# Capped attention and two expert layers on one core: attention in units of two key blocks, the shared block on half rows, seven pairs in float32

## The chip, the core and the metric

The kernel runs on one core of a Trainium2 chip. Its engines work side by side, each through its own queue in order: TensorE (PE, with its weight loads shown apart as PEld), VectorE (DVE), ScalarE (ACT), GpSimd (POOL) and SyncE (SP, which here issues the DMAs). The metric is the device time of one launch in microseconds.

## What is computed

```python
def _attn_ref(q, k, v, cap):                       # q, k, v: (2, 12, 448, 64)
    scores = np.matmul(q, k.transpose(0, 1, 3, 2)) / np.sqrt(64)
    scores = cap * np.tanh(scores / cap)
    attn = np.exp(scores - np.max(scores, axis=-1, keepdims=True))
    attn = attn / (np.sum(attn, axis=-1, keepdims=True) + 1e-09)
    return np.matmul(attn, v)
...
x = attn_out.transpose(0, 2, 1, 3).reshape(896, 768)
h = np.maximum(np.maximum(x @ w1, x @ w2), x @ w3)  # 768 x 768 each
y = h @ w_out
g = y @ w_in                                        # 768 x 2048
g = np.maximum(g, 0.0) + alpha * np.minimum(g, 0.0)
return g @ w_out2                                   # 2048 x 768
```

All is float32. The weights come as pairs of 32-bit words and are decoded on the chip.

## The kernel before

**Heads go in pairs.** The 24 heads are 12 pairs. In `qk` a pair's two heads lie on partitions 0 to 63 and 64 to 127, so that a score product of one head takes 64 rows of the array and the two heads' products lie beside each other. The 448 keys are cut into three blocks of 128 for both heads and one shared block: its 128 rows are the last 64 keys of the first head and, below, the last 64 of the second. `CHUNKS` (L142) lists 12 x 4 chunks: blocks 0, 1, 2 and the shared one (`None`).

**A chunk's steps.** `scores` (L251) makes the transposed scores (keys on partitions, 448 queries along the row) in a PSUM tile `sc`, two buffers, in three passes of rounded parts: high by high, high by low, low by high. `tanh` (L263) reads it on ACT into the tile `a`; `exp` (L269) works on `a` in place. No maximum is subtracted, since the cap bounds the scores. `weighted` (L284) multiplies with v: the stationary operand is 128 keys x 128 columns, 64 of v and 64 of ones, so that the same product gives the sum of the exponentials. In the pairs of `FULL` (L144: 1, 3, 5, 7, 9, 11) this is one float32 matmul for each head, which the trace shows as two instructions; in the other pairs `a` and v are split into a rounded part and a remainder (`a_high`, `a_low`, `v_high`, `v_low`, on DVE) and three passes are made. In the shared block each head's product takes all 128 rows, and zeros, written once by `beside` (L212), stand in v against the other head's keys.

**After a pair.** `taken` copies the two products from PSUM on ACT (`e`); `summed`, `inverted`, `in_row` and `spread` bring the sums by DMA into a column, invert them, and spread them over 64 partitions (`rc`, `row`, `rb`); `normal`, `x_high` and `x_low` give the normalised result, split in two parts, to the expert layers.

**Order.** Every step is a task with an engine, an estimated cost, what it must follow, and a key (`KEYS`, L186, in chunks from the chunk's number). `planned` (L146) goes through the tasks with these costs and emits them in the order of the planned start times; `in_order` then fixes that order for every queue. Buffers: `AB` 6 tiles `a`, `SB` and `LB` 4 tiles for the split parts, `PB` 2 PSUM tiles each for scores and products. Three weight blocks of the first expert layer are loaded and decoded inside attention (`GATES`, L184). Then `experts` (L511) begins with ten of the twelve pairs for all three weight blocks and takes the last two pairs at the end (`late`).

**The rest**, some 400 us, is matmuls of rounded parts in three passes (`product`, L94).

Of the kernel before, what the change touches and what calls it, by code (L numbers as in the profile page):

```python
# [10 lines left out]
F32 = mybir.dt.float32  # L11
F32R = mybir.dt.float32r
# [3 lines left out]
AF = mybir.ActivationFunctionType  # L16
# [14 lines left out]
def attention_moe_moe2(ctx: ExitStack, tc: tile.TileContext, t):  # L31
# [6 lines left out]
    KF, _, DM = t["w_in2"].shape  # L38
    KD = DM // P

    AB, SB, LB, PB = 6, 4, 4, 2

    WARM = 11

# [96 lines left out]

    CHUNKS = [(p, block) for p in range(PAIRS) for block in (0, 1, 2, None)]  # L142

    FULL = range(1, PAIRS, 2)  # L144

    def planned(tasks, start):  # L146

# [45 lines left out]
    def fast_attention(xh, xl, pools, begin):  # L193
# [78 lines left out]
        def a_high(i):  # L272
            a = splits[i]
            ah = work.tile([P, 2, S], F32R, name="ah", bufs=SB)[:, : a.shape[1]]
            rounded(ah, a, "DVE")
            splits[i] = a, ah

        def a_low(i):
            a, ah = splits[i]
            al = work.tile([P, 2, S], F32R, name="al", bufs=LB)[:, : a.shape[1]]  # L280
            remainder(al, a, ah)
            splits[i] = ah, al

        def weighted(i):  # L284
# [4 lines left out]
            for head in range(2):  # L289
                j = 0 if block is None else head  # L290
                out = pvs[p][:, head, :S]
                start, stop = block == 0, block is None
                cols = slice(head * P, (head + 1) * P)
                if p in FULL:
                    nc.tensor.matmul(out, values(p, "f")[:, c, cols], splits[i][:, j], start=start, stop=stop)  # L295
                    continue
                ah, al = splits[i]
                vh, vl = (values(p, part)[:, c, cols] for part in "hl")
                nc.tensor.matmul(out, vh, ah[:, j], start=start, stop=False)  # L299
                nc.tensor.matmul(out, vh, al[:, j], start=False, stop=False)  # L300
                nc.tensor.matmul(out, vl, ah[:, j], start=False, stop=stop)  # L301

        def taken(p, h):

            if h == 0:
                divisors[p] = small.tile([P, 2, S], F32, name="e"), small.tile([CP, 2, S // CP], F32, name="rc")
            nc.scalar.copy(out=divisors[p][0][:, h], in_=pvs[p][:, h, :S])  # L307

        def summed(p, h):
# [57 lines left out]
        splitting = [i for i in range(n) if CHUNKS[i][0] not in FULL]  # L367
        of = [[i for i in range(n) if CHUNKS[i][0] == p] for p in range(PAIRS)]
# [5 lines left out]
        for p in range(PAIRS):  # L374
# [4 lines left out]
            if p == 0:  # L379
                for x, (cols, dep) in enumerate(((slice(0, CUT), "KIN"), (slice(CUT, QK), "QIN"))):  # L380
                    m = cols.stop - cols.start
                    add(("XKH", 0, x), "DVE", rounding("DVE", m), [((dep, 0), 0.0)], -99 + x, qk_high, 0, cols, "DVE")
                    add(("XKL", 0, x), "DVE", low(m), [("XKH", 0, x)], -98.5 + x, qk_low, 0, cols)
            else:
                transfer(("Lx", p), 0.63, 2.6, past("XKL", p - 2, 0), s0 + KEYS["Lx"], load_qk, p)
                free = past("SC", of[p - 2][-1]) if p > 1 else []
# [9 lines left out]
            if not full:  # L396
# [5 lines left out]
            for i in of[p]:  # L402
                two = CHUNKS[i][1] is not None
                m = S * (2 if two else 1)
                deps = past("SC", i - 1) + past("TA", i - PB)
                deps += [("XKL", 0, 0 if i == 0 else 1)] if p == 0 else [("XKL", p, 0)]
                add(("SC", i), "PE", 0.75 if two else 0.61, deps, i + KEYS["SC"], scores, i)
                old = i - AB
                free = [] if old < 0 else past("PV", old) if CHUNKS[old][0] in FULL else past("AL", old)
                add(("TA", i), "ACT", 0.9 if two else 0.53, [("SC", i)] + free, i + KEYS["TA"], tanh, i)  # L410
                add(("EX", i), "ACT", 0.93 if two else 0.56, [("TA", i)], i + KEYS["EX"], exp, i)
                if full:
                    deps = [("EX", i)]
                    cost = 1.5
                else:
                    x = splitting.index(i)
                    free = past("PV", splitting[x - SB]) if x >= SB else []
                    add(("AH", i), "DVE", rounding("DVE", m), [("EX", i)] + free, i + KEYS["AH"], a_high, i)
                    free = past("PV", splitting[x - LB]) if x >= LB else []
                    add(("AL", i), "DVE", low(m), [("AH", i)] + free, i + KEYS["AL"], a_low, i)  # L420
                    deps = [("AL", i)]
                    cost = 1.22
                deps = deps + ready_v + past("PV", i - 1)
                deps += past("TKA", p - 2) + past("TKB", p - 2)
                add(("PV", i), "PE", cost, deps, i + KEYS["PV"], weighted, i)
# [15 lines left out]
        for w, gate in enumerate(GATES):  # L441
            stages = begin(w)
            step = lambda stages=stages: next(stages, None)
            free = [("EX", gate)]
            transfer(("WL", w), 0.4, 4.2, [("EX", max(0, gate - 8))] + past("W2", w - 2), 1000 + w * 10, step)
            times = (("ACT", 0.8), ("DVE", 1.05), ("DVE", 1.8), ("ACT", 0.8), ("DVE", 0.9))
            for j, (engine, cost) in enumerate(times):
                deps = [(("WL!", w), 0.3)] + free + past("W4", w - 2) if j == 0 else [(f"W{j - 1}", w)]
                add((f"W{j}", w), engine, cost, deps, 1000 + w * 10, step)
        anchors = {}  # L450
        for name in planned(tasks, 3.6):
            task, args = tasks[name][4]
            task(*args)
            if name in (("EX", n - 1), ("AL", splitting[-1]), ("PV", n - 1), ("DA", PAIRS - 1)):
                anchors[name[0]] = list(nc.cur_bb.bb.instructions)[-1]
        return list(anchors.values())

# [249 lines left out]
```

## Time and profile before

| | us |
|---|---|
| median of 3 runs (539.97 to 541.96) | 541.27 |
| the profiled execution, device time | 541.33 |
| its span in the trace | 539.3 |
| first score matmul | 6.08 |
| the attention's last product on PE ends, first expert matmul | about 117.9 |
| last wait of PE for attention's results ends | 137.87 |

The profile is of one execution. A row of the timeline gives start, duration, engine, line, operation, tiles, shape and how many equal instructions are merged; in brackets stands the idle time before it and what ended it. Matmuls are pipelined: a matmul's duration in the trace is longer than its share of the engine, so that share is read from the distances of starts.

### The profile page before, as it was taken

Reading aid. Unit: us, or ns where it says so; the run is one execution under the profiler, and the core shown is the slowest. Engines: PE = TensorE matmul, PEld = TensorE weight load, DVE = VectorE, ACT = ScalarE, POOL = GpSimd, SP = SyncE. Lnnn points to the kernel's source line nnn. Section 1 sums busy time; section 2 is a strip of 40 time slices with the busy share of each in tenths; the row PEclk is TensorE's granted clock in tenths of the full one; section 3 lists DMA queues with packets and bytes.
Section 4 is the critical chain, followed back from the end, with each engine's and each line's share of the span. In section 5 each row is a group of like instructions: output and inputs, shape, how many; then the busy total and the mean of one; then the engine's idle time right before and its main releaser. Section 6 shows DMA issues by size and latency. Waiting matters only on the chain.

```text
span 539.3 us, 6459 instructions
## 1 busy us (share of the span) xinstructions
PE 527.0 (98%) x2519; PEld 447.4 (83%) x2519; DVE 380.6 (71%) x512; ACT 233.2 (43%) x296; POOL 5.0 (1%) x20
## 2 busy tenths in 40 slices
PE   7999999999999999999999999999999999999995
PEld 3665566579899999999999999999999999999994
DVE  5768899754988767667666899999988665565300
ACT  5989999862444333233333233333333223223110
POOL 3000000000000000000000000000000000000000
PEclk9999999999999999999999999999999999999998
DMA  6456244115355332233333233322333344344001
GB/s 198 139 152 175 69 115 108 36 35 153 117 177 175 118 117 95 93 110 113 118 117 108 68 118 117 117 80 98 108 98 107 108 131 143 107 132 141 1 35 40
DMA packets 27350, 59.19 MB, mean 110 GB/s; under 512 B 14384, under 2 KB 17584, under 8 KB 27312
## 3 DMA queue, kind: packets, MB, share of 16 engines
q1 hardware_dynamic: 27312, 58.69, 35.3%
q8 instruction: 22, 0.36, 0.3%
q14 instruction: 16, 0.13, 0.1%
HBM read 55.85 MB, written 2.80 MB: 109 GB/s over the span
## 4 chain that ended last, share of the span: by engine, by line
PE 88%; ACT 4%; DVE 3%; DMA 2%; issue 1%; DVEq 0%; SPq 0%; ACTq 0%
PE acc L99 25%; PE acc L100 24%; PE acc L98 24%; PE pv L295 5%; PE sc L260 5%; PE pv L299 2%; ACT a L266 2%; PE pv L300 1%; PE pv L301 1%; DMA rb<-row 1%; ACT a L270 1%; DVE rb L336 1%; ACT e L307 1%; DMA cap_t<-in_cap 1%; DVE f L115 1%
## 5 line engine op out<-in xcount | busy, mean ns | idle before, releaser
L82 ACT CAST wh<-f 128x768 fp32r<-128x768 f32 (+1 forms) x58 | 47.2, 814 | 203.4 <-PE acc L99 195.2
L87 DVE TENSOR_TENSOR wl<-f,wh 128x768 fp32r<-128x768 f32 (+1 forms) x58 | 53.6, 925 | 52.5 <-ACT wh L82 52.3
L99 PE MATMUL acc<-xl,wh 128*128 128x448 f32 x216 | 79.0, 366 | 0.7 <-DVE xl L87 0.7
L98 PE MATMUL acc<-xh,wh 128*128 128x448 f32 x216 | 79.2, 367 | 0.0
L100 PE MATMUL acc<-xh,wl 128*128 128x448 f32 x216 | 78.9, 365 | 0.0
L108 ACT ACTIVATE f<-raw 128x768 f32<-128x768 f32 (+1 forms) x58 | 51.1, 881 | 55.0 <-DVE wl L87 39.1
L98 PE MATMUL acc<-yh,wh 128*128 128x448 f32 x192 | 70.7, 368 | 0.0
L99 PE MATMUL acc<-yl,wh 128*128 128x448 f32 x192 | 70.7, 368 | 0.0
L100 PE MATMUL acc<-yh,wl 128*128 128x448 f32 x192 | 70.7, 368 | 0.0
L98 PE MATMUL acc<-gh,wh 128*128 128x448 f32 x192 | 70.7, 368 | 0.0
L99 PE MATMUL acc<-gl,wh 128*128 128x448 f32 x192 | 70.7, 368 | 0.0
L100 PE MATMUL acc<-gh,wl 128*128 128x448 f32 x192 | 70.7, 368 | 0.0
L118 DVE SCALAR_TENSOR_TENSOR f<-raw,f 128x768 int32<-128x768 int32 (+1 forms) x58 | 53.9, 929 | 1.7
L115 DVE SCALAR_TENSOR_TENSOR f<-raw,f 128x768 int32<-128x768 int32 (+1 forms) x58 | 53.8, 928 | 1.4
L110 DVE TENSOR_SCALAR f<-f 128x768 f32<-128x768 f32 (+1 forms) x58 | 31.6, 545 | 25.5 <-ACT f L108 25.5
L266 ACT ACTIVATE a<-sc,s_in 128x896 f32<-128x896 f32 (+1 forms) x48 | 43.7, 918 | 9.6 <-PE sc L260 9.2
L270 ACT ACTIVATE a<-a,cap_t 128x896 f32<-128x896 f32 (+1 forms) x48 | 44.9, 955 | 0.4
L99 PEld LDWEIGHTS acc<-xl,wh 128*128 128x128 f32 x216 | 40.6, 188 | 4.5 <-DVE xl L87 1.1
L98 PEld LDWEIGHTS acc<-xh,wh 128*128 128x128 f32 x216 | 40.6, 188 | 3.4 <-PE pv L295 0.2
L100 PEld LDWEIGHTS acc<-xh,wl 128*128 128x128 f32 x216 | 40.6, 188 | 3.2
L295 PE MATMUL pv<-a,vf 128*128 128x448 f32 x96 | 40.5, 553 | 0.0
L99 PEld LDWEIGHTS acc<-yl,wh 128*128 128x128 f32 x192 | 36.0, 188 | 3.7
(70 smaller groups left out, 757.6 us busy)
## 6 DMA issues: line engine op xcount, KB each, us to landing
raw<-in_w SPq DMA_DIRECT2D x18, 768.0 KB, 4.4
raw<-in_w_in SPq DMA_DIRECT2D x16, 768.0 KB, 4.3
raw<-in_w_out SPq DMA_DIRECT2D x12, 768.0 KB, 4.4
raw<-in_w_out SPq DMA_DIRECT2D x12, 640.0 KB, 3.9
qkd<-in_qk SPq DMA_DIRECT2D x11, 480.0 KB, 3.8
rb<-row SPq DMA_DIRECT2D x24, 112.0 KB, 3.0
out<-ot SPq DMA_DIRECT2D x12, 224.0 KB, 2.8
vd<-in_v SPq DMA_DIRECT2D x6, 256.0 KB, 4.2
```

The lines of the kernel that those rows point to most:

```text
L82: nc.scalar.copy(out=hi, in_=src)
L87: nc.vector.tensor_tensor(out=lo, in0=src, in1=hi.bitcast(F32), op=ALU.subtract)
L98: nc.tensor.matmul(out, wh, xh, start=first and i == 0, stop=False)
L99: nc.tensor.matmul(out, wh, xl, start=False, stop=False)
L100: nc.tensor.matmul(out, wl, xh, start=False, stop=last and i == n - 1)
L108: nc.scalar.activation(out=f, in_=high.bitcast(F32), func=AF.Abs)
L110: nc.vector.tensor_scalar(out=f, in0=f, scalar1=WORD_MIN, scalar2=WORD_MAX, op0=ALU.max, op1=ALU.min)
L115: nc.vector.scalar_tensor_tensor(out=fi, in0=low, scalar=29, in1=fi, op0=ALU.logical_shift_right, op1=ALU.bitwise_or)
L118: nc.vector.scalar_tensor_tensor(out=fi, in0=high, scalar=-0x40000000, in1=fi, op0=ALU.bitwise_and, op1=ALU.bitwise_or)
L266: nc.scalar.activation(out=a, in_=sc, func=AF.Tanh, scale=s_in)
L270: nc.scalar.activation(out=splits[i], in_=splits[i], func=AF.Exp, scale=cap_t)
L295: nc.tensor.matmul(out, values(p, "f")[:, c, cols], splits[i][:, j], start=start, stop=stop)
```

## The change

Two neighbouring chunks become a unit: blocks 0 and 1 (four score tiles wide) and block 2 with the shared block (three wide). There are 24 units.

- The tile `a` is four wide. `tanh` still runs by chunk. `exp`, the split of `a` and the products with v run by unit; in the first two and the last two units (`FINE`) the exponentials and the products of the first chunk are steps of their own (`EA`, `PA`).
- The scores of a unit's second chunk get a key that puts them right behind those of the first.
- In the shared block each head's product with v takes only the 64 rows of its own keys, and the heads take turns. The zeros in v, and the four memsets of 64x64 in `h` and `f` for each buffer set, go.
- `FULL` becomes 0, 1, 3, 5, 7, 9, 11: pair 0 is no longer split.
- Buffers are halved in number (`AB` 3, `SB`, `LB` 2) and doubled in size; `e` and `rc` get three buffers, and `taken` follows the normalisation of the pair three before instead of two.
- Keys, gates and estimated costs are stated in units.

```diff
-    AB, SB, LB, PB = 6, 4, 4, 2
+    AB, SB, LB, PB = 3, 2, 2, 2
...
-    FULL = range(1, PAIRS, 2)
+    UNITS = [4, 3] * PAIRS
+    FINE = (0, 1, len(UNITS) - 2, len(UNITS) - 1)
+    FULL = [0, 1, 3, 5, 7, 9, 11]
...
-    GATES = (20, 27, 44)
+    GATES = (10, 13, 22)
     KEYS = dict(
-        Lx=-16, Lv=-12, XKH=-6, XKL=-5, VH=-3, VL=-2.5, TKA=4.2, TKB=4.3, INV=7, NM=8, XH=8.5, XL=9,
-        SC=-1.5, TA=-1, EX=0.5, AH=0.6, AL=0.7, PV=4,
+        Lx=-8, Lv=-6, XKH=-4, XKL=-3.9, VH=-1.5, VL=-1.2, TKA=1.9, TKB=2, INV=2.2, NM=2.7, XH=2.9, XL=3.2,
+        SC=-1.4, TA=-0.5, EX=0, AH=0.1, AL=0.2, PV=1.25,
     )
...
-            if part != "l":
-                nc.gpsimd.memset(v_[D:, 3, D : 2 * D], 0.0)
-                nc.gpsimd.memset(v_[:D, 3, 2 * D : 3 * D], 0.0)
...
         def tanh(i):
             sc = scs.pop(i)
-            a = work.tile([P, 2, S], F32, name="a", bufs=AB)[:, : sc.shape[1]]
-            nc.scalar.activation(out=a, in_=sc, func=AF.Tanh, scale=s_in)
-            splits[i] = a
+            if i % 2 == 0:
+                splits[i // 2] = work.tile([P, 4, S], F32, name="a", bufs=AB)
+            at = i % 2 * 2
+            nc.scalar.activation(out=splits[i // 2][:, at : at + sc.shape[1]], in_=sc, func=AF.Tanh, scale=s_in)
-        def exp(i):
-            nc.scalar.activation(out=splits[i], in_=splits[i], func=AF.Exp, scale=cap_t)
+        def exp(u, cols):
+            a = splits[u][:, cols]
+            nc.scalar.activation(out=a, in_=a, func=AF.Exp, scale=cap_t)
...
+            at = i % 2 * 2
+            if p in FULL:
+                terms = [(values(p, "f"), splits[i // 2])]
+            else:
+                (vh, vl), (ah, al) = (values(p, part) for part in "hl"), splits[i // 2]
+                terms = [(vh, ah), (vh, al), (vl, ah)]
+            def term(m, head):
+                v_, a_ = terms[m]
+                r = slice(head * D, (head + 1) * D) if block is None else slice(0, P)
+                j = at if block is None else at + head
+                start, stop = block == 0 and m == 0, block is None and m == len(terms) - 1
+                v_ = v_[r, c, head * P : (head + 1) * P]
+                nc.tensor.matmul(pvs[p][:, head, :S], v_, a_[r, j], start=start, stop=stop)
+            turns = [(m, head) for m in range(len(terms)) for head in range(2)]
+            for m, head in turns if block is None else sorted(turns, key=lambda x: x[1]):
+                term(m, head)
...
+                for i in (2 * u, 2 * u + 1):
+                    deps = past("SC", i - 1) + past("TA", 2 * u - 2) + past("TA", 2 * u - 1)
...
+                    add(("SC", i), "PE", cost, deps, u + KEYS["SC"] - i % 2 * 1000, scores, i)
...
+                if u in FINE:
+                    add(("EA", u), "ACT", 0.93, [("TA", 2 * u)], u + KEYS["EX"] - 0.3, exp, u, slice(0, 2))
+                cols = slice(2 if u in FINE else 0, UNITS[u])
+                cost = 0.17 + (cols.stop - cols.start) * S / 1200
+                add(("EX", u), "ACT", cost, [("TA", 2 * u), ("TA", 2 * u + 1)], u + KEYS["EX"], exp, u, cols)
...
+                if u in FINE:
+                    first_deps = [("EA", u)] + deps[1:]
+                    add(("PA", u), "PE", 1.6, first_deps, u + KEYS["PV"] - 0.2, weighted, chunks[:1])
+                    deps, chunks, cost = [("EX", u), ("PA", u)], chunks[1:], cost - 1.5
+                add(("PV", u), "PE", cost, deps, u + KEYS["PV"], weighted, chunks)
-            free = past("NA", p - 2) + past("NB", p - 2)
+            free = past("NA", p - 3) + past("NB", p - 3)
...
```

## Rows read from the trace of the kernel before

**Rows 1.** The profile's page: busy time by engine, and the chain that ended last.

```profile
PE 527.0 (98%) x2519; PEld 447.4 (83%) x2519; DVE 380.6 (71%) x512; ACT 233.2 (43%) x296; POOL 5.0 (1%) x20
PE 88%; ACT 4%; DVE 3%; DMA 2%; issue 1%; DVEq 0%; SPq 0%; ACTq 0%
```

**Rows 2.** Busy time by stage: stretch, length, PE, PEld, DVE, ACT, POOL, PE clock, DMA, GB/s.

```profile
6.08:117.90 111.82, 107.62 (x493) 67.68 (x493) 89.54 (x146) 99.81 (x131) 3.55 (x12) 1.00 0.43 118
117.90:137.90 20.00, 19.26 (x96) 17.50 (x94) 12.21 (x23) 5.65 (x10) 0.00 (x0) 1.00 0.51 153
137.90:538.00 400.10, 395.27 (x1922) 360.64 (x1922) 277.61 (x340) 126.29 (x154) 0.00 (x0) 1.00 0.33 106
```

**Rows 3.** Timeline of PE: start, duration, instruction; a float32 pair, and attention's end.

```profile
63.58 0.36 PE L260 MATMUL sc<-qkh,qkl 128*128 128x448 f32 x1
63.78 1.66 PE L295 MATMUL pv<-a,vf 128*128 128x448 f32 x4
65.38 0.47 PE L260 MATMUL sc<-qkh 64*128 64x448 f32 x2
65.69 0.37 PE L260 MATMUL sc<-qkl,qkh 64*128 64x448 f32 x2
65.89 0.36 PE L260 MATMUL sc<-qkh,qkl 64*128 64x448 f32 x2
66.18 1.77 PE L295 MATMUL pv<-a,vf 128*128 128x448 f32 x4
...
68.19 0.36 PE L260 MATMUL sc<-qkl,qkh 64*128 64x448 f32 x2
...
111.92 6.17 PE L295 MATMUL pv<-a,vf 128*128 128x448 f32 x16
...
118.13 0.36 PE L99 MATMUL acc<-xl,wh 128*128 128x448 f32 x1
```

**Rows 4.** Timeline of PE: its waits in attention, and first and last change of shape.

```profile
9.58 0.47 PE L260 MATMUL sc<-qkh 128*128 128x448 f32 x1
...
14.47 0.47 PE L260 MATMUL sc<-qkl,qkh 64*128 64x448 f32 x2 [0.50 <-DVE qkl L87]
...
78.14 0.47 PE L260 MATMUL sc<-qkh 128*128 128x448 f32 x1 [0.71 <-ACT a L266]
...
88.34 0.47 PE L260 MATMUL sc<-qkh 128*128 128x448 f32 x1 [0.89 <-ACT a L266]
...
106.36 0.47 PE L299 MATMUL pv<-ah,vh 128*128 128x448 f32 x1 [0.27 <-ACT e L307]
```

**Rows 5.** Timeline of ACT: exponentials of both widths and what follows them.

```profile
60.08 1.97 ACT L270 ACTIVATE a<-a,cap_t 128x896 f32<-128x896 f32 x2
61.95 0.99 ACT L266 ACTIVATE a<-sc,s_in 128x896 f32<-128x896 f32 x1
62.84 0.83 ACT L82 CAST wh<-f 128x768 fp32r<-128x768 f32 x1
...
75.61 0.68 ACT L270 ACTIVATE a<-a,cap_t 128x448 f32<-128x448 f32 x1
76.16 0.58 ACT L82 CAST xh<-rb 128x448 fp32r<-128x448 f32 x1
```

**Rows 6.** Waits of ACT from 6 to 118 us: in total, times, longest.

```profile
ACT a L266 <- PE sc L260: 9.2, 13, 3.3
```

**Rows 7.** First v load in float32: its issue on SP, and DMA issues of 0 to 30 us.

```profile
7.30 1.35 SPq L227 DMA_DIRECT2D vf<-in_v  x2
vf<-in_v SPq DMA_DIRECT2D x4, 128.0 KB, 4.8
```

**Rows 8.** Timeline of ACT and PE where the last two pairs are handed over.

```profile
110.75 1.65 ACT L270 ACTIVATE a<-a,cap_t 128x896 f32<-128x896 f32 x2
...
121.07 0.96 ACT L307 COPY e<-pv 128x448 f32<-128x448 f32 x2
137.87 0.47 PE L99 MATMUL acc<-xl,wh 128*128 128x448 f32 x1 [0.74 <-DVE xl L87]
```

More of the change, by code (lines that the diff above doesn't have):

```diff
@@ L264, in tanh, with a_high, a_low, weighted @@
             sc = scs.pop(i)
-            a = work.tile([P, 2, S], F32, name="a", bufs=AB)[:, : sc.shape[1]]
-            nc.scalar.activation(out=a, in_=sc, func=AF.Tanh, scale=s_in)
-            splits[i] = a
-        def exp(i):
-            nc.scalar.activation(out=splits[i], in_=splits[i], func=AF.Exp, scale=cap_t)
-        def a_high(i):
-            a = splits[i]
-            ah = work.tile([P, 2, S], F32R, name="ah", bufs=SB)[:, : a.shape[1]]
+            if i % 2 == 0:
[5 more added lines that the diff above has]
+            nc.scalar.activation(out=a, in_=a, func=AF.Exp, scale=cap_t)
+        def a_high(u):
+            a = splits[u][:, : UNITS[u]]
+            ah = work.tile([P, 4, S], F32R, name="ah", bufs=SB)[:, : UNITS[u]]
             rounded(ah, a, "DVE")
[L276 to L280, printed above, removed]
+            splits[u] = a, ah
+        def a_low(u):
+            a, ah = splits[u]
+            al = work.tile([P, 4, S], F32R, name="al", bufs=LB)[:, : UNITS[u]]
             remainder(al, a, ah)
-            splits[i] = ah, al
-        def weighted(i):
+            splits[u] = ah, al
+        def weighted(chunks):
+            for i in chunks:
+                chunk_weighted(i)
+        def chunk_weighted(i):
             p, block = CHUNKS[i]
@@ L288, in weighted @@
             c = 3 if block is None else block
[L289 to L301, printed above, removed]
+            at = i % 2 * 2
[14 more added lines that the diff above has]
+                term(m, head)
         def taken(p, h):
             if h == 0:
-                divisors[p] = small.tile([P, 2, S], F32, name="e"), small.tile([CP, 2, S // CP], F32, name="rc")
+                e = small.tile([P, 2, S], F32, name="e", bufs=3)
+                divisors[p] = e, small.tile([CP, 2, S // CP], F32, name="rc", bufs=3)
             nc.scalar.copy(out=divisors[p][0][:, h], in_=pvs[p][:, h, :S])
@@ L366, in fast_attention @@
         n = len(CHUNKS)
-        splitting = [i for i in range(n) if CHUNKS[i][0] not in FULL]
-        of = [[i for i in range(n) if CHUNKS[i][0] == p] for p in range(PAIRS)]
+        splitting = [u for u in range(n // 2) if CHUNKS[2 * u][0] not in FULL]
+        of = [[u for u in range(n // 2) if CHUNKS[2 * u][0] == p] for p in range(PAIRS)]
         for name in ("KIN", "QIN"):
@@ L385, in fast_attention @@
                 transfer(("Lx", p), 0.63, 2.6, past("XKL", p - 2, 0), s0 + KEYS["Lx"], load_qk, p)
-                free = past("SC", of[p - 2][-1]) if p > 1 else []
+                free = past("SC", 2 * of[p - 2][-1] + 1) if p > 1 else []
                 engine, cols = ROUND["QK"], slice(0, QK)
@@ L401, in fast_attention @@
                 ready_v = [("VL", p)]
[L402 to L416, printed above, removed]
+            for u in of[p]:
+                even, m = u % 2 == 0, S * UNITS[u]
+                for i in (2 * u, 2 * u + 1):
+                    deps = past("SC", i - 1) + past("TA", 2 * u - 2) + past("TA", 2 * u - 1)
+                    deps += [("XKL", 0, 0 if i == 0 else 1)] if p == 0 else [("XKL", p, 0)]
+                    cost = 0.71 if CHUNKS[i][1] in (0, 1) else 0.6 if i % 2 == 0 else 0.8
+                    add(("SC", i), "PE", cost, deps, u + KEYS["SC"] - i % 2 * 1000, scores, i)
+                old = u - AB
+                free = [] if old < 0 else past("PV", old) if CHUNKS[2 * old][0] in FULL else past("AL", old)
+                for i in (2 * u, 2 * u + 1):
+                    two = CHUNKS[i][1] is not None
+                    deps = [("SC", i)] + free
+                    add(("TA", i), "ACT", 0.9 if two else 0.53, deps, u + KEYS["TA"] + i % 2 * 0.01, tanh, i)
+                if u in FINE:
[3 more added lines that the diff above has]
+                add(("EX", u), "ACT", cost, [("TA", 2 * u), ("TA", 2 * u + 1)], u + KEYS["EX"], exp, u, cols)
+                if not full:
+                    x = splitting.index(u)
@@ L417, in fast_attention @@
                     free = past("PV", splitting[x - SB]) if x >= SB else []
-                    add(("AH", i), "DVE", rounding("DVE", m), [("EX", i)] + free, i + KEYS["AH"], a_high, i)
+                    add(("AH", u), "DVE", rounding("DVE", m), [("EX", u)] + free, u + KEYS["AH"], a_high, u)
                     free = past("PV", splitting[x - LB]) if x >= LB else []
-                    add(("AL", i), "DVE", low(m), [("AH", i)] + free, i + KEYS["AL"], a_low, i)
-                    deps = [("AL", i)]
@@ L422, in fast_attention @@
-                    cost = 1.22
-                deps = deps + ready_v + past("PV", i - 1)
+                    add(("AL", u), "DVE", low(m), [("AH", u)] + free, u + KEYS["AL"], a_low, u)
+                cost = (3.1 if even else 2.7) if full else (2.5 if even else 2.25)
+                deps = [("EX" if full else "AL", u)] + ready_v + past("PV", u - 1)
                 deps += past("TKA", p - 2) + past("TKB", p - 2)
-                add(("PV", i), "PE", cost, deps, i + KEYS["PV"], weighted, i)
@@ L426, in fast_attention @@
-            free = past("NA", p - 2) + past("NB", p - 2)
+                chunks = [2 * u, 2 * u + 1]
+                if u in FINE:
[4 more added lines that the diff above has]
+            free = past("NA", p - 3) + past("NB", p - 3)
@@ L444, in fast_attention @@
             free = [("EX", gate)]
-            transfer(("WL", w), 0.4, 4.2, [("EX", max(0, gate - 8))] + past("W2", w - 2), 1000 + w * 10, step)
+            transfer(("WL", w), 0.4, 4.2, [("EX", max(0, gate - 4))] + past("W2", w - 2), 1000 + w * 10, step)
             times = (("ACT", 0.8), ("DVE", 1.05), ("DVE", 1.8), ("ACT", 0.8), ("DVE", 0.9))
@@ L453, in fast_attention @@
             task(*args)
-            if name in (("EX", n - 1), ("AL", splitting[-1]), ("PV", n - 1), ("DA", PAIRS - 1)):
+            if name in (("EX", n // 2 - 1), ("AL", splitting[-1]), ("PV", n // 2 - 1), ("DA", PAIRS - 1)):
                 anchors[name[0]] = list(nc.cur_bb.bb.instructions)[-1]
```

## The prediction, made before the changed kernel ran

> **What bounds the kernel now.** I read the page's busy shares and its chain first: PE is busy for 98% of the span and holds 88% of the chain that ended last [rows 1]. Then the stages: the change touches the first 111.8 us of work, attention from 6.08 to 117.9; the 400 us behind 137.9 are the same instructions and nearly all PE (395.3 busy) [rows 2]. So what attention saves on PE comes off the end one for one, if the handover at 118 to 138 us lets it. PE's clock is granted at 1.00, its 2.4 GHz level, in every stage [rows 2]; it gets no term. But ACT is close behind: 99.8 us busy in the same 111.8, with DVE at 89.5 [rows 2]. A saving on PE beyond some 10 us would only be met by ACT.
>
> What PE's time consists of is read from distances of starts. A matmul of rounded parts on all rows takes 0.20 (63.58 to 63.78), and two on half rows, one for each head, take 0.20 together (65.69 to 65.89) [rows 3]. A float32 matmul is two instructions; sixteen of these fill 111.92 to 117.93 (the start of the second expert matmul, 118.13, less 0.20), so 0.376 each, 0.75 a matmul [rows 3]. Between shapes there is a surcharge: from 63.78 to 65.69 lie four float32 instructions (1.50), one pair of scores (0.20) and 0.21 more; from 65.89 to 68.19 lie two score pairs (0.40), 1.50 of products and 0.40 for two changes of shape [rows 3]. A change between half rows and all rows therefore costs 0.20. Going along PE's timeline I count 57 of them, the first at 9.58, the last at 106.36 [rows 4]; three a pair on the way in and three on the way out would be 72, and where two score chunks or two products stand together some are saved.
>
> Before: scores 48 chunks x 3 x 0.20 = 28.8; split products 6 pairs x 8 x 3 x 0.20 = 28.8; float32 products 6 x 8 x 0.75 = 36.0; shapes 57 x 0.20 = 11.4. Sum 105.0. The stage is 111.8, so 6.8 are waits: three later ones for ACT make 1.9 (0.71, 0.89, 0.27), and most of the other 4.9 lies before 15 us, where the first products wait for the split and the next scores for their remainder, and three later waits for ACT (0.71, 0.89, 0.27) [rows 4].
>
> **The change part by part.**
>
> *Shared block on half rows.* In a split pair six matmuls on all rows become three pairs on half rows: 1.20 becomes 0.60, as in the scores; 5 pairs save 3.0. In float32 no row shows half rows. The heads take turns, but each matmul is two instructions, so the order is A1 A2 B1 B2, and with starts in order only A2 and B1 can lie beside each other: 3 x 0.376 = 1.13 instead of 1.50. The bounds are 0.75 (both heads wholly together) and 1.50 (one after the other); the nearest row is the score pair, which shows that two row halves run together, so I take 1.13 and save 0.37 in each of 7 pairs, 2.6 (0 to 5.2). What speaks for more is a rule of the Trainium skill, page "TensorEngine Tiling (Array Packing)", section Overview, Theoretical Speedup: it gives up to 2x for a contraction of 64 rows or fewer. By it the block would be 0.75 and the sum 2.6 better; no row here shows it for float32.
>
> *Pair 0 in float32.* On all rows its products go from 4.8 to 6.0 us: plus 1.2. (Its half-row saving is counted above as one of the seven.) DVE loses pair 0's splits; it is not on the path in the steady part.
>
> *Units.* Scores of a unit stand together, and so do its products. Even units have scores on half rows and products on all rows; odd ones have scores first on half, then on all rows, products first on all, then on half rows. With scores and products of units alternating, that is four changes of shape a pair whichever way they pair up, 48 instead of 57: minus 9 x 0.20 = 1.8. The four fine units and places where the order doesn't alternate can move this by a few in either direction; bounds 40 to 60, that is plus or minus 2.
>
> *PE in sum:* scores 28.8, split 5 x (18 x 0.20 + 0.60) = 21.0, float32 7 x (4.50 + 1.13) = 39.4, shapes 9.6: 98.8, which is 6.2 less (3.6 to 8.8 by the half rows alone).
>
> *Exponentials by unit.* Two of width 896 take 1.87, so 0.935 each (60.08 to 61.95), one of width 448 takes 0.55 (75.61 to 76.16) [rows 5]; the part that doesn't grow is 2 x 0.55 - 0.935 = 0.165. Twenty units merge two exponentials: minus 3.3 us on ACT. No row has a wider one; if width were free of that gain, ACT stays as it was, at worst 0. ACT goes to 96.5 busy. Tanh by chunk costs what it did (0.89) [rows 5]. What follows the exponential now comes later in the unit: the first chunk's products wait for the second chunk's tanh and the double exponential, some 1.7 us more. The order lets products run over a unit behind the scores, so PE has other products meanwhile; without that cover it costs 1.7 x 20. That is the rival below.
>
> *Start.* The products of pair 0 no longer wait for DVE, but for v in float32. That load must follow a memset on POOL and stands on SP as two issues; such a pair was issued at 7.30 and took 4.8 us from issue to landing in this stretch [rows 7], so it lands at 12.1 to 12.8. Four fewer memsets ahead gain at most half a microsecond of it. Behind these two issues on SP stand the later loads of q, k and v, which have buffers and time. The fine units let the products begin after the first exponential. Today PE is in step again at about 15 us [rows 4]. I take plus 0.5, between minus 1.5 (the DVE chain gone) and plus 1.5 (the load late).
>
> *Buffers, keys, gates.* The bytes stay the same; three buffers of `e` take away a wait of `taken`; weight blocks are decoded at the same place in the work. Nothing, with ACT's slack as cover.
>
> *Handover.* The copies of the last pair start at 121.07, and PE takes their result at 137.87 after waiting 0.74 [rows 8]; the ten early pairs give 90 x 0.20 = 18 us of cover. If the copies move up with PE's end, the wait stays. But ACT's last exponentials (110.75) [rows 8] move up by ACT's 3.3, not by PE's 6.2; what hangs on ACT could then be up to 2.9 later against PE. I take plus 0.3 (minus 0.7 to plus 2.9).
>
> **Sum.** Minus 6.2 plus 0.5 plus 0.3 is minus 5.4. The profiled execution took 541.33 for a span of 539.3, 0.06 above the median, so its rows stand for the median: 541.3 - 5.4 = 535.9. ACT would be 96.5 of 106.4 us, 91% instead of 89%: tight, but no more than it was to within 2 points.
>
> **The rivals.**
>
> *PE and ACT in step by units (slower).* Products of a unit are up to 3.0 us of PE in one piece, twice today's 1.5. Scores that come free just behind such a piece wait for 3.0 + 0.2, then take 0.6 and 0.2 for the shape, and 0.2 or so pass to ACT: 4.2 us. From that moment ACT has one tanh (0.9), the exponential (1.5 on average) and copies and casts (some 0.75 a unit): 3.15. So up to 1.0 us a unit would be open on ACT. Today ACT waits for scores 9.2 us in 13 waits, the longest 3.3 at the start [rows 6], 0.25 a unit without it. With 96.5 busy, 3.5 at both ends and x a unit in 24 units, the stage is 100 + 24x: slower from x = 0.5. At 0.8 it is 119, plus 7.4: 548.7. Against it: scores have the earlier key and two buffers, and the waits today are small although ACT is at 89%. Also for it, the Trainium skill, "TensorEngine Tiling (Array Packing)", Performance Considerations, PSUM Bottleneck: tiling makes TensorE faster, not the emptying of PSUM, which may then bind. Rows 2 agree so far that ACT, which empties the scores, has 12 us to spare. Chance 0.11.
>
> *Float32 on half rows doesn't overlap.* The shared block stays at 1.50: minus 2.8 in all, 538.5. Chance 0.15.
>
> *It overlaps wholly.* Minus 8.0, 533.3. Chance 0.10.
>
> *Given back in order and handover.* The saving on PE is there, but ACT, now 91% loaded, makes three or four more waits of 0.9 as in rows 4, or the handover takes its 2.9: 538.8. Chance 0.16.
>
> **How the numbers follow.** The forecast has 0.48. Its own range is 533 to 538.5. The range goes down to 531 (whole overlap with two of today's waits gone) and up to 541.5, where the two small-gain cases overlap each other; that leaves out the rival in step and little else. A measurement of this kernel tells about 0.5%, 2.7 us, from no change, so faster means below 538.6: 0.45 of the forecast, the 0.10, half of the no-overlap case and a third of the giving-back case: 0.68. Slower is the rival in step with 0.01 for worse: 0.12. The same is 0.20.
>
> **What would show it.** Half rows: in the new timeline the shared block's four float32 instructions take 1.1 us between starts; 0.75 or 1.5 decides the two rivals. Shapes: about 48 changes at 0.20. Exponentials of width 1792 with about 1.7 us, 1344 with 1.3. ACT's waits for scores in total: near 9 for the forecast, above 16 for the rival in step. The wait ahead of the late expert matmuls: below 3.7. First product at 12 to 13 us. Wrong if attention's end doesn't move from 117.9 to about 112, or if PE's idle start grows until its clock falls below 1.00.

## The result, and the profile after

The changed kernel takes 531.5 us (median of six runs, 528.6 to 536.7) against 540.6 (six runs, 539.0 to 542.2) for the kernel before: a ratio of 0.985, interval 0.980 to 0.990. The forecast was 535.9, so it was faster, as forecast. On the chip of e1 below the medians are 532.0 and 536.5: 4.5 apart, where they are 9.1 apart here. Behind attention the same 2016 expert matmuls take 408.3 us from the second start to the last in some profiled executions and up to 414.7 in others, at a granted clock of 1.00 in all and with the same program both ways (after 413.8, e1 408.3), so below the lengths of the attention stage are compared rather than single totals.

The profiled execution took 533.62 us for a span of 532.2 (before: 541.33 and 539.3). The page of after, busy time and chain, answers [rows 1]:

```profile
PE 518.1 (97%) x2511; PEld 442.1 (83%) x2511; DVE 372.1 (70%) x482; ACT 228.9 (43%) x276; POOL 3.9 (1%) x12
PE 96%; ACT 1%; DMA 1%; DVE 0%; issue 0%; DVEq 0%; ACTq 0%
```

The stages of after (stretch, length, PE, PEld, DVE, ACT, POOL, PE clock, DMA, GB/s), for [rows 2]:

```profile
6.07:110.46 104.39, 99.76 (x485) 62.63 (x486) 80.86 (x116) 95.97 (x112) 2.38 (x5) 0.98 0.48 128
110.46:129.53 19.07, 19.07 (x95) 17.47 (x95) 12.28 (x23) 5.14 (x8) 0.00 (x0) 1.00 0.53 148
129.53:532.10 402.57, 395.30 (x1923) 360.68 (x1922) 277.69 (x340) 126.35 (x154) 0.00 (x0) 1.00 0.33 106
```

Attention is 7.46 us shorter (from 117.93 - 6.08 = 111.85, the end taken in the same way as here, to 104.39). The early expert matmuls are 0.93 shorter than the 20.00 of before. The last matmul starts 8.34 earlier, and 1.2 of that isn't in the span, because what follows the last matmul's start took 7.7 us in this execution and 6.5 before. PE's clock in attention is 0.98, not 1.00. Over the whole span this execution has the highest granted clock of the six (0.994; the median is 0.989), so its attention may be shorter than the usual one.

The timeline of PE in after (start, duration, instruction, the wait before it in brackets), for [rows 3], [rows 4] and [rows 8]:

```profile
12.26 0.48 PE L261 MATMUL sc<-qkh 64*128 64x448 f32 x2 [1.87 <-ACT a L270]
...
13.67 3.27 PE L311 MATMUL pv<-a,vf 128*128 128x448 f32 x8
...
18.39 2.62 PE L311 MATMUL pv<-a,vf 128*128 128x448 f32 x8
20.49 0.71 PE L261 MATMUL sc<-qkh 64*128 64x448 f32 x2
21.04 0.36 PE L261 MATMUL sc<-qkl,qkh 64*128 64x448 f32 x2
...
36.09 0.48 PE L311 MATMUL pv<-ah,vh 64*128 64x448 f32 x2
36.41 0.36 PE L311 MATMUL pv<-al,vh 64*128 64x448 f32 x2
...
64.72 0.47 PE L261 MATMUL sc<-qkh 64*128 64x448 f32 x2 [2.07 <-ACT a L270]
...
66.90 0.57 PE L311 MATMUL pv<-ah,vh 128*128 128x448 f32 x1
67.28 0.57 PE L311 MATMUL pv<-al,vh 128*128 128x448 f32 x1
...
69.20 0.36 PE L311 MATMUL pv<-al,vh 128*128 128x448 f32 x1
69.41 0.37 PE L311 MATMUL pv<-ah,vl 128*128 128x448 f32 x1
...
110.35 0.47 PE L98 MATMUL acc<-xh,wh 128*128 128x448 f32 x1
110.66 0.37 PE L99 MATMUL acc<-xl,wh 128*128 128x448 f32 x1
...
129.53 0.47 PE L99 MATMUL acc<-xl,wh 128*128 128x448 f32 x1
```

The piece from 18.39 holds a unit's end in a float32 pair: two products on all rows, then the shared block as four instructions on half rows. From its start to the second pair of scores at 21.04 are 2.65. The two products take 1.50, the change of shape 0.20, the first pair of scores 0.20: 0.75 is left for the shared block, half of what it took on all rows. Two narrow stretches of the same timeline (20.06 to 20.40 and 20.63 to 20.70) show how:

```profile
19.98 0.65 PE L311 MATMUL pv<-a,vf 64*128 64x448 f32 x2
...
20.46 0.54 PE L311 MATMUL pv<-a,vf 64*128 64x448 f32 x2
```

The block's four instructions start two by two, at 19.98 and at 20.46, where those on all rows go one by one, 0.376 apart; of the 0.48 between the two starts some 0.10 is the change of shape. The second two end after 0.54, as long as a single one on all rows (median 0.54). So two lie beside each other each time, read here as one of either head. All seven float32 blocks of after start so. In a split pair the three pairs on half rows go at 0.20 or, the first behind a change of shape, 0.32 (36.09, 36.41), as the scores do.

PE stands still twice for about 2 us, at 12.26 and at 64.72. Behind the second pause a matmul takes 0.38 (66.90 to 67.28) where it takes 0.21 at 69.20 (to 69.41). The stretch from 66 to 67 shows why (same columns as the stages): the granted clock is 0.50, its 1.2 GHz level.

```profile
66.00:67.00 1.00, 1.00 (x4) 0.87 (x4) 1.00 (x2) 1.00 (x2) 0.00 (x0) 0.50 0.60 152
```

What the pause at 64.72 waits for, and the handover, are in the timeline of ACT in after:

```profile
60.75 1.42 ACT L274 ACTIVATE a<-a,cap_t 128x1344 f32<-128x1344 f32 x1
62.08 0.51 ACT L322 COPY e<-pv 128x448 f32<-128x448 f32 x1
62.49 0.83 ACT L82 CAST wh<-f 128x768 fp32r<-128x768 f32 x1
63.22 0.53 ACT L322 COPY e<-pv 128x448 f32<-128x448 f32 x1
63.65 1.92 ACT L270 ACTIVATE a<-sc,s_in 128x896 f32<-128x896 f32 x2
...
111.12 0.83 ACT L82 CAST wh<-f 128x768 fp32r<-128x768 f32 x1 [3.21 <-DVE f L118]
111.86 0.53 ACT L322 COPY e<-pv 128x448 f32<-128x448 f32 x1
...
112.78 0.53 ACT L322 COPY e<-pv 128x448 f32<-128x448 f32 x1
```

Two copies of `e` and the rounding of the first weight block stand between an exponential and the tanh that frees the scores' buffer; PE has finished the products it has and can't write scores. At the end the last pair's copies start 1.4 us behind attention's end (111.86 against 110.46), where they started 3.1 behind it before (121.07 against 117.93, [rows 8]).

ACT's exponentials (by shape: busy, mean ns) and ACT's waits for scores (total, times, longest) in after, for [rows 5] and [rows 6]:

```profile
L274 ACT ACTIVATE a<-a,cap_t 128x1792 f32<-128x1792 f32 x10 | 18.0, 1796 | 0.2
L274 ACT ACTIVATE a<-a,cap_t 128x1344 f32<-128x1344 f32 x10 | 14.2, 1419 | 0.3
```

```profile
ACT a L270 <- PE sc L261: 5.3, 3, 3.3
```

ACT is busy for 92% of the shorter stage, and without the 3.3 at the start it waits 2.0 for scores where it waited 5.9 before. After PE it is the busiest engine; that it would bind next isn't shown (e5 and e11 take work off it without gain).

### The profile page after: what moved, and what is told of

Same layout as the page of the kernel before. It is cut to its first block, busy times and chain, and to the rows that moved or that the text cites. A ratio compares the mean times of both kernels' runs of the same rounds, so it can differ in the third digit from the quotient of the medians.

```text
span 532.2 us, 6370 instructions
## 1 busy us (share of the span) xinstructions
PE 518.1 (97%) x2511; PEld 442.1 (83%) x2511; DVE 372.1 (70%) x482; ACT 228.9 (43%) x276; POOL 3.9 (1%) x12
## 4 chain that ended last, share of the span: by engine, by line
PE 96%; ACT 1%; DMA 1%; DVE 0%; issue 0%; DVEq 0%; ACTq 0%
PE acc L98 26%; PE acc L99 26%; PE acc L100 26%; PE pv L311 12%; PE sc L261 6%; ACT a L270 1%; DMA cap_t<-in_cap 1%; ACT a L274 0%; ACT e L322 0%; DVE qkl L87 0%; ACT wh L82 0%; DVE qkh L84 0%; ACT ot L584 0%; DVEq L78 0%; DVE cap L53 0%
## 5 line engine op out<-in xcount | busy, mean ns | idle before, releaser
L270 ACT ACTIVATE a<-sc,s_in 128x896 f32<-128x896 f32 (+1 forms) x48 | 41.9, 919 | 5.5 <-PE sc L261 5.3
L311 PE MATMUL pv<-a,vf 128*128 128x448 f32 (+1 forms) x112 | 41.1, 557 | 0.0
L274 ACT ACTIVATE a<-a,cap_t 128x1792 f32<-128x1792 f32 (+3 forms) x28 | 39.5, 1422 | 0.5
L98 PEld LDWEIGHTS acc<-yh,wh 128*128 128x128 f32 x192 | 36.0, 188 | 3.7
```

What stands on the lines that cost most here:

```text
L98: nc.tensor.matmul(out, wh, xh, start=first and i == 0, stop=False)
L270: nc.scalar.activation(out=splits[i // 2][:, at : at + sc.shape[1]], in_=sc, func=AF.Tanh, scale=s_in)
L274: nc.scalar.activation(out=a, in_=a, func=AF.Exp, scale=cap_t)
L311: nc.tensor.matmul(pvs[p][:, head, :S], v_, a_[r, j], start=start, stop=stop)
```

## The experiments

Each run names its ratio to the kernel before on the same chip. "Stage" is the time from the first score to the first expert matmul in the profiled execution, 111.85 before and 104.39 after. "Lost to the half clock" sums what the granted clock lacks to 1.00 over stretches of 1 us in that stage: 1.7 in after. It says how much slower PE ran there, not how much longer the stage was.

**e1. The changed kernel again.** No edit.

> The changed kernel itself, to be beside the others on one chip. Theory 'products': 8.3 us below the kernel before, as in its trace, with the last expert matmul some 8 us earlier. The theory that its gain is mostly luck of one chip expects under 3 us here. Its profile shows again a wait of PE for ACT's tanh near 62 to 65 us of about 2 us, followed by matmuls at 0.37 us (granted clock 0.50) for some 3 us, if that pause belongs to the order of the work; elsewhere, or not at all, if it was this one execution's.

Measured: 532.0 us, ratio 0.987 [0.979, 0.995], stage 109.0. The medians are 4.5 apart, not the 8.3 of the first theory. The second pause is there again, 2.98 here, and both pauses are followed by the half clock; 5.1 is lost to it. The stage, and in the timeline of PE the second pause:

```profile
6.11:115.12 109.01, 102.96 (x485) 64.35 (x486) 81.00 (x116) 96.09 (x112) 2.37 (x5) 0.95 0.46 123
```

```profile
68.15 0.74 PE L261 MATMUL sc<-qkh 64*128 64x448 f32 x2 [2.98 <-ACT a L270]
```

So the same program's stage differs by 4.6 between two executions, mostly at the two pauses: 3.4 more are lost to the half clock, and ACT, which waits 5.3 for scores in the one, waits 8.0 in the other. The granted clock of this execution, 0.988 over the span, is near the median of the six in the result (0.989), so its stage may be the more usual of the two.

**e2. Shared block on all rows again**, the rest of the change kept.

```diff
-                r = slice(head * D, (head + 1) * D) if block is None else slice(0, P)
+                r = slice(0, P)
```

(and the two memsets of zeros back.)

> The changed kernel with the shared block's products on all 128 rows again (and the zeros in v again), nothing else changed, the planned order and costs the same. Theory 'whole overlap': the float32 block goes from 0.75 to 1.50 in seven pairs (5.25) and the split one from 0.6 to 1.2 in five (3.0), changes of shape stay near 49: 8.2 us longer on PE, so about as slow as the kernel before, within 1.5. Theory 'staggered' of the prediction (block 1.13): 2.6 plus 3.0, 5.6 longer. Rival 'ACT is the bound': with ACT at 96 of 104 us the half rows give only what ACT leaves, 3 us or less.

Measured: 534.2 us, 0.994 [0.990, 0.997]; stage 109.4 without any half clock in it. Its chain (start, us, what), first a float32 pair, then a split one, and behind it the same pieces of after:

```profile
17.07 1.60 PE sc L264 x9
18.67 3.01 PE pv L314 x8
21.68 1.43 PE sc L264 x12
23.11 3.20 PE pv L314 x8
...
30.93 1.43 PE sc L264 x12
32.35 2.63 PE pv L314 x12
34.98 1.63 PE sc L264 x9
36.61 2.40 PE pv L314 x12
```

```profile
16.94 1.60 PE sc L261 x9
18.55 2.46 PE pv L311 x8
21.00 1.21 PE sc L261 x11
22.22 3.20 PE pv L311 x8
...
29.48 1.21 PE sc L261 x11
30.70 2.66 PE pv L311 x12
33.35 1.61 PE sc L261 x7
34.97 2.01 PE pv L311 x12
```

A float32 pair takes 9.24 here and 8.47 in after, a split one 8.09 and 7.49: 0.77 and 0.60 saved. Over 7 and 5 pairs that is 8.4. The stage less its waits in brackets and its half clock says much the same: 109.44 - 4.52 = 104.9 here and 104.39 - 5.68 - 1.7 = 97.0 in after, 7.9 apart. The heads' float32 halves overlap wholly. With the forecast's half overlap it would be 7 x 0.37 + 3.0 = 5.6. But in time half rows are worth only 2 to 4 us (534.2 against 532.0; ratios 0.994 and 0.987 on this chip), which is what the rival expected and not the 8.2 of the first theory. The profiled stages of e1 and of this run are only 0.4 apart: PE comes to its pauses earlier in e1, waits 1.7 more there and loses 5.1 to the half clock, which isn't in this run. The rival's reason, a full ACT, isn't what the traces show: ACT is busy for 96.1 of 109.0 in e1 and 96.8 of 109.4 here.

**e3. Exponentials by chunk again.**

```diff
-            a = splits[u][:, cols]
-            nc.scalar.activation(out=a, in_=a, func=AF.Exp, scale=cap_t)
+            parts = [cols] if cols.stop - cols.start <= 2 else [slice(0, 2), slice(2, cols.stop)]
+            for some in parts:
+                a = splits[u][:, some]
+                nc.scalar.activation(out=a, in_=a, func=AF.Exp, scale=cap_t)
```

> The changed kernel with every unit's exponential in two instructions, one for each chunk, planned order the same. ACT gets 20 x 0.165 = 3.3 us more work. Theory 'products' (PE sets the stage): at most 1 us longer than the changed kernel. Rival 'ACT is the bound': the whole 3.3 us or more, with waits of PE for tanh grown by as much.

Measured: 531.4 us, 0.988 [0.983, 0.993]; stage 106.6 with 3.4 lost to the half clock. ACT is busy 97.8, 1.8 more than in after, about half of the 3.3 expected. No difference shows in the time; the stage is 2.2 longer than the profiled one of after and 2.4 shorter than the second one. Between these the runs can't tell what merging is worth.

**e4. The kernel before with half rows alone.** Line 288 and on take the new order of the shared block; units, pair 0, buffers and gates stay.

```diff
+                r = slice(head * D, (head + 1) * D) if block is None else slice(0, P)
...
+                v_ = v_[r, c, head * P : (head + 1) * P]
```

> The kernel before with the half rows alone: six float32 pairs, chunks as before. Theory 'products': float32 saves 6 x 0.75 = 4.5, split 6 x 0.6 = 3.6, changes of shape between 2 fewer and as many as the 57: 8 us faster than the kernel before, so that the units give next to nothing. Rival 'ACT sets the bound without the merged exponentials': ACT's 99.8 us of work in a stage of 104 leaves no room for its 12 us of waiting, so only about 4 us faster.

Measured: 535.2 us, 0.994 [0.990, 0.999]; stage 109.7. The half-row products now stand beside half-row scores, so there are 40 changes of shape instead of 57, and PE's work is 28.8 + 6 x 4.20 + 6 x 5.25 + 40 x 0.20 = 93.5, 11.5 less than before. Only 2.1 of it come out. PE's waits in it (total, times, longest):

```profile
PE sc L257 <- ACT a L263: 5.0, 6, 2.0
PE sc L257 <- DMA qkd<-in_qk: 1.5, 1, 1.5
```

Waits in attention sum to 9.8, where before has 4.3 in brackets, and 3.4 are lost to the half clock. So a faster PE alone gives most of it back as waits, in an order of work that was planned for the slower one. With the rest of the change (fewer instructions on ACT and DVE, pair 0, a third buffer, its own order) PE has more work, 96.2 (see below), and the ratios are still lower, 0.985 and 0.987, though their intervals touch or overlap this one's. What the rest gives, it gives by letting more of the saving through.

**e5. Rounding of `x` on DVE.** Takes the `xh` casts off ACT.

```diff
-    ROUND = dict(QK="DVE", V="DVE", X="ACT")
+    ROUND = dict(QK="DVE", V="DVE", X="DVE")
```

> The changed kernel with the rounding of the normalised result (x_high) on DVE instead of ACT: ACT loses 12 x 0.46 = 5.5 us, DVE gains about 12 x 0.4; the plan follows. Theory 'ACT paces the stage and its spare time decides PE's pauses': the wait of PE for tanh in the 60s falls from 2 to 3 us to under 1, no half-clock stretch follows it, attention ends 2 to 4 us earlier than in the changed kernel's runs, 104.4 and 109.0 long, at 101 to 102.5. Rival 'the pause is the plan's order, not ACT's load': the wait stays near 2 us or turns up elsewhere, and the stage stays 104 to 109.

Measured: 535.9 us, 0.992 [0.988, 0.996]; stage 108.6, with 5.1 lost to the half clock. The first theory fell, and the rival held. ACT is busy 2.7 less (93.3), DVE 4.2 more (85.1), and the pause turns up on DVE, where the split of the exponentials is now late; the longest of PE's waits:

```profile
PE pv L311 <- DVE al L87: 2.5, 1, 2.5
```

Giving ACT's work to DVE doesn't take the pause away: at this place, where a split pair follows a float32 one, PE needs both.

**e6. The pause at the start filled.** Seven matmuls on zeros, 0.21 each, behind the fourth chunk of scores.

```diff
+            if i == 4:
+                fill = pvps.tile([P, 2, 512], F32, tag="ps", name="fill")
+                for _ in range(7):
+                    nc.tensor.matmul(..., fills[:, 0], zeros_in, start=True, stop=True)
```

> The changed kernel with seven idle matmuls (products of zeros, 0.21 us each) put into PE's pause of 1.88 us between the fourth and the fifth score chunk; nothing waits for them. Theory 'the half-clock stretch follows from the pause': no matmul at 0.37 us follows at 12 to 17 us in any profile, and the median falls by about 1 us, a half-clock stretch of 3 us costing 1.5 to 2 where it occurs. Rival 'the stretch has another cause': granted clock at 12 to 17 us falls as before, in some runs, and the time is unchanged.

Measured: 533.2 us, 0.987 [0.981, 0.992]; stage 104.5. At 12 to 17 us the clock stays at 1.00 and the wait is 0.35; the later pause (2.08) and its half clock remain, as in the profile of after. The pause at the start can be bought off, but the time isn't told from the changed kernel's.

**e7. Two buffers of `e` and `rc`**, and the copies behind the pair two before, as before the change.

```diff
-                e = small.tile([P, 2, S], F32, name="e", bufs=3)
+                e = small.tile([P, 2, S], F32, name="e")
...
-            free = past("NA", p - 3) + past("NB", p - 3)
+            free = past("NA", p - 2) + past("NB", p - 2)
```

> The changed kernel with two buffers of e and rc instead of three, and the copies after the normalisation of the pair two before, as in the kernel before. Theory 'the third buffer mended the handover': the wait ahead of the late expert matmuls comes back, 0.7 us or more, and the copies of the last pair start again some 3 us after the last product; about 1 us slower. Rival 'the handover only moved up with attention's end': no wait there, time within 0.5 us.

Measured: 535.3 us, 0.993 [0.990, 0.996]; stage 107.9. Products wait 3.1 for the copies (1.48 at 65.83, 0.47, 1.18), and the late expert matmuls wait again, 2.1 us at 136.57:

```profile
PE pv L311 <- ACT e L322: 3.1, 3, 1.5
PE acc L98 <- ACT xh L82: 2.1, 1, 2.1
```

The third buffer, put at nothing in the prediction, is worth some 3 to 4 us (ratio 0.993 against the changed kernel's 0.985 and 0.987, whose intervals touch or overlap this one's) and holds the handover.

**e8. Six float32 pairs**, pair 0 split as before.

```diff
-    FINE = (0, 1, len(UNITS) - 2, len(UNITS) - 1)
-    FULL = [0, 1, 3, 5, 7, 9, 11]
+    FINE = (len(UNITS) - 2, len(UNITS) - 1)
+    FULL = [1, 3, 5, 7, 9, 11]
```

> The changed kernel with pair 0 split again (six float32 pairs; its units then not fine). By PE's work alone 1.05 us less (4.2 for 5.25). Theory 'pair 0 in float32 buys a better start': first product later than 13.7 us or more waits before 20 us, by more than 1 us, so that attention ends no earlier. Rival 'pair 0 in float32 only costs': attention ends 1 us earlier.

Measured: 536.4 us, 0.991 [0.987, 0.995]; stage 108.3. PE's first products wait for the split (2.17 at 12.55, 1.70 at 14.96) and two later ones do (1.1 each), 3.4 are lost to the half clock behind the start; DVE is busy 86.8 instead of 80.9. Up to 20 us the waits and the half clock come to 8.2 here, 3.6 in after and 4.5 in e1. So pair 0 in float32 saves more at the start than the 1.05 us that it costs on PE; in the time the intervals overlap.

**e9. Both pauses filled.** Seven idle matmuls as above, nine more in pair 6, ahead of chunk 26's scores.

```diff
+    IDLE = {4: (0, 7), 26: (6, 9)}
```

> The changed kernel with idle matmuls (products of zeros) in both of its pauses of PE: seven after the fourth score chunk and nine ahead of the third score chunk of pair 6, in the PSUM tile that the pair's products overwrite afterwards; the order of all other work stays. Theory 'the half-clock stretches follow from the two pauses': granted clock 1.00 through attention in the profile, stage at 102 to 103 us (104.4 less its 1.9 of half clock, 109.0 less 6.0), mean clock of the executions above that of the changed kernel (about 0.989) by 0.004 or more, and the median 2 to 4 us below the changed kernel's against the same kernel before. Rival: waits elsewhere take it back; the stage stays above 104.

Measured: 533.2 us, 0.988 [0.983, 0.993]. Stage; then the nine idle matmuls and the scores behind the pause:

```profile
6.05:111.01 104.96, 102.17 (x501) 62.90 (x502) 80.97 (x116) 96.13 (x112) 2.38 (x5) 1.00 0.48 127
```

```profile
57.58 2.11 PE L261 MATMUL pv<-fills 128*128 128x512 bf16 x9
...
66.50 0.48 PE L269 MATMUL sc<-qkh 64*128 64x448 f32 x2 [1.50 <-ACT a L278]
```

The clock is 1.00 throughout, and the stage is 105.0, not 102 to 103: the rival's side. But the nine matmuls ran ahead of the pause, not in it. They put off the scores behind them, so the tanh that frees the buffer came later too, and 1.50 of the pause stayed. The 1.9 us that they take (nine at 0.21) are as much as the 1.7 lost to the half clock in the profile of after. The mean granted clock of the six executions rose to 0.995, as expected (0.989 in after and in e1), but the ratio is the changed kernel's. So keeping the clock up in this way buys nothing that the time shows; whether a pause shortened at its source would, the run doesn't tell.

**e10. The first weight block one gate earlier**, start filled as above.

```diff
-    GATES = (10, 13, 22)
+    GATES = (9, 13, 22)
```

> With the seven idle matmuls at the start and the first weight block decoded one unit earlier (after the exponential of unit 9 instead of 10), so that its rounding on ACT doesn't stand between the copies of pair 5 and the tanh of pair 6. Theory 'ACT's extra work at that place makes the second pause': the wait near 64 us falls from 2.1 to under 1.3 us without any idle matmul there, and no half-clock stretch follows. Rival 'PE would run dry there anyway, since the split pair's products wait for DVE': a wait of 2 us or more stays at the same place.

Measured: 531.3 us, 0.987 [0.980, 0.992]; stage 105.6. The clock is 1.00 throughout, but PE waits 2.26 at 65.56, now for DVE's `al`, and for three shorter ones behind. The pause isn't the weight block's alone.

**e11. Rounding of the early weight blocks on DVE**, start filled as above.

```diff
-        rounded(hi, f, "ACT")
+        rounded(hi, f, engine)
```

> With the seven idle matmuls at the start and the rounding of the three weight blocks on DVE inside attention: ACT loses 3 x 0.74 us there, DVE gains 3 x 0.5. Theory 'ACT's extra work makes the second pause': the wait near 64 us falls to about 1.3 (2.1 less 0.74), the stage to 101 to 103. Rival 'DVE is the one that is late': the wait stays or moves to the products of a split pair, as with the other rounding on DVE.

Measured: 535.2 us, 0.986 [0.979, 0.993]; stage 106.0. The wait, still for tanh, is 1.83 at 65.72 instead of 2.08 in e6; it doesn't go away, and 1.7 is lost to the half clock behind it.

None of these is measurably better than the changed kernel.

## Why the prediction was right, point by point

*The bound: true at best.* The prediction took PE's saving in attention to come out one for one, as long as ACT has room. PE's work went from 105.0 to 28.8 + 21.0 + 7 x 5.25 + 48 x 0.20 = 96.2, that is 8.8 less (48 changes of shape, counted as the 57 of before). In the profile of after 7.46 of it come out: what is left of the stage, waits and half clock, is 8.2, 1.4 more than before's 6.8. With 0.9 from the handover that is -8.8 + 1.4 - 0.9 = -8.3, against a forecast of -6.2 + 0.5 + 0.3 = -5.4. (That it meets the 8.34 seen at the last matmul proves nothing, since 1.4 is what was left over.) In e1 the same saving makes the stage only 2.8 shorter, and in e4 a saving of 11.5 makes it 2.1 shorter. In e1 ACT is busy for 88% of the stage, in after for 92%, so the saving wasn't met by a full ACT. It went into PE's pauses and the half clock behind them, much as in the rival "given back in order and handover" (0.16).

*The number: right, in part by luck.* Two errors pull against each other. PE saved 2.6 more than forecast (8.8 against 6.2), and waits and half clock took back 1.4 in one execution and 6.0 in the other, where the sum had 0.5. The two stages are 7.5 and 2.8 shorter, 5.1 in the mean, near the forecast. That the median lies 4.4 below the forecast doesn't show a larger gain: the expert matmuls, which the change doesn't touch, differ by more between two executions of the same program (413.8 and 408.3).

*Half rows in float32: the step that was mis-sized.* 1.13 was taken and 0.75 measured, in the timeline and again with the block back on all rows. The prediction's argument, that starts in the order A1 A2 B1 B2 let only the middle two overlap, fails: the four instructions start two by two (19.98, 20.46), read as one of either head each time. That is 7 x 0.38 = 2.7, all of the 2.6 by which PE's sum was short. It was the rival of whole overlap, put at 0.10; its 533.3 is 1.8 from the median. The sentence that spoke for it, on the Trainium skill's "TensorEngine Tiling (Array Packing)", Overview, Theoretical Speedup (up to 2x for 64 rows or fewer), agrees with the trace for float32: 1.50 to 0.75.

*Split half rows* saved 3.0 as forecast (0.60 a pair). *Shapes*: 48 changes, as forecast, at 0.20. But it isn't the units that bring them down: half rows in the old order have 40 (e4), and units on all rows 43 (e2). *Pair 0* wasn't measured by itself on PE; what it buys at the start shows in the run with six float32 pairs.

*Exponentials.* 1.80 and 1.42 long, and from start to start, as the forecast's 1.7 and 1.3 were meant, some 1.7 and 1.33 (60.75 to 62.08); ACT was busy 96.0 against 96.5. That unit-wise waits don't put PE and ACT in step held: ACT waited 5.3 for scores, not above 16.

*Start.* The first product came at 13.67, forecast 12 to 13: it stands behind a chunk of scores that waits 1.87 for tanh. Its load of v is hardly earlier: in e10, with that pause filled, the product waits 0.24 for v and starts at 13.97. In the profile of after the waits outside the second pause and its half clock are 8.2 - 2.1 - 1.7 = 4.4, some 0.5 less than before's 4.9; in e1 the half clock takes 1.7 at the start. Plus 0.5 lies between.

*Handover: wrong sign.* Plus 0.3 was taken, -0.9 measured. The last pair's copies do move up with PE's end, and further, since the third buffer of `e` lets the pair before it leave at 105.57; the late wait fell from 0.74 to some 0.1 (129.53, without a bracket). The prediction had put buffers at nothing; two buffers bring 2.1 us of wait back.

*Not foreseen:* the pauses at 12 and at 62 to 68 us, and the half clock behind them. The prediction named a clock below 1.00 as a sign that it would be wrong at the start; the clock fell there in e1 and not in the profile of after. This is where part of the larger saving went: of 8 us less work on PE, half rows gave 2 to 4 in the time (e2 against e1). The Trainium skill, "TensorEngine Tiling (Array Packing)", Performance Considerations, PSUM Bottleneck, says that the emptying of PSUM may bind once tiling has made TensorE faster; the trace agrees at these two places (1.87 and 2.07 us), where the scores wait for a buffer that ACT has yet to empty.

*Open:* why one execution has the half clock behind a pause and another not, and how the stage divides between ACT, DVE and the half clock once both pauses are gone. Work moved off ACT made waits on DVE in e5 and left the wait for tanh in e11, an earlier gate (e10) made one on DVE, and no run gave room on both.

## What to carry to other kernels

A contraction with zeros in half its rows is worth splitting into two half-row matmuls also in float32, where it halved the time here; count the changes of shape, which the order of the work decides (40 to 57 here). When the bounding engine gets faster by 8%, give the next one its buffers at the same time: the third `e` was worth about as much in time as the half rows, 3 to 4 us against 2 to 4. Don't book the engine's saving one for one: of 8.8 us, 7.5 came out in one execution and 2.8 in another. And look for pauses of 2 us in an otherwise dense stage, because the half clock behind them can cost as much again.

## What the runs showed of the hardware

- Two float32 matmuls of 448 columns on the two row halves take 0.75 us together, one on all rows 0.75 alone; their instructions start two by two (19.98 and 20.46 in after).
- A change between 64-row and 128-row matmuls costs 0.20 us. The Trainium skill, "TensorEngine Tiling (Array Packing)", Key Properties, has a change of mode drain TensorE; the trace agrees in that a change costs time, and gives the size.
- A pause of about 2 us can be followed by 3 to 7 us at 0.50 of the clock. At the start that followed a pause of 1.88 or 1.89 in e1, e3, e5 and e7, but not one of 1.88 in e2 or of 1.87 in after; later it followed 2.07 in after, but not 2.26 in e10. With idle matmuls on zeros in the first pause the clock stayed at 1.00 there each time (e6, e9, e10, e11).
- From some 130 us behind attention's end the expert matmuls go at 0.2027 or at 0.2067 from start to start in different executions, at a granted clock of 1.00 in both; in e4 they go at 0.2067 up to there and at 0.2027 behind. The cause isn't shown.
